# Two gate and up tiles move from the attention's filler to the seven-product phase, with a two-rate filler and later stores

## The chip, the cores and the metric

The kernel runs on one core of a Trainium2 chip. The core has a tensor engine (PE in the profile, with its weight loads as PEld), a vector engine (DVE), a scalar engine (ACT), GpSimd (POOL), and SyncE (SP), whose queue issues nearly all DMAs here. Each engine works through its own instructions in the order written and waits on semaphores for the others. The metric is device microseconds of one execution, the median of several runs; lower is better.

## The reference

One transformer block with a sequence of 2048 and a width of 640, in float32. Normalised tokens go through a causal attention with a window of 256 (32 heads of 20) and, in parallel, through a gated feed-forward part of width 1728; both are added to the input.

```python
xn = _layernorm(x, axis=-1)
return x + _A_ref(xn, A_wqkv, A_wo) + _B_ref(xn, B_w_gate, B_w_up, B_w_down)
...
scores = jnp.einsum("bhqd,bhkd->bhqk", q, k) * (Dh ** -0.5)
mask = (idx[:, None] - idx[None, :] >= 0) & (idx[:, None] - idx[None, :] < W)
p = _softmax(jnp.where(mask[None, None], scores, -1e9), axis=-1)
o = jnp.einsum("bhqk,bhkd->bhqd", p, v)
...
g = jnp.einsum("bsd,df->bsf", x, w_gate)
u = jnp.einsum("bsd,df->bsf", x, w_up)
return jnp.einsum("bsf,fd->bsd", _gelu(g) * u, w_down)
```

## The kernel before

Every large product is done with float32 operands split into a high and a low part, so that one product of depth 640 takes 3 x 5 = 15 matmuls of 128x128 weights against 512 tokens (`dense_steps`, L107; its matmuls are L111). The tokens stand in four chunks of 512 (`c` = 0 to 3). The work falls into four stretches.

First the normalisation and transposition, with the first query and key tiles and values. Then the attention, in 32 units: unit `u` is four heads (group `g = u // 4`) by one chunk (`c = u % 4`). Then the seven-product phase, which computes gate and up tiles. Last the output products.

The attention is written as a hand-made order (`attention`, L822). A unit has 14 slots. In each slot the program first does what was put off to that slot (`defer`), then what the tables say: pairs of row maxima at slots 0, 4 and 8 (`BURSTS`, `max_pair`, tile `ps_m`), score tiles and their exponentials at slots 2, 4, 6, 8 and 10 (`SCORES`, `exp_piece`, tiles `ps_e` and `P`), at slot 0 the product of the previous unit's probabilities with the values (`av_unit`, tile `ps_o`), and at slots 9 and 12 the loads of keys and queries for the unit three later (`load_stack`, tiles `ks` and `qs`). The queries of unit `u + 3` are first read by the maxima at slot 4 of the next unit, six slots after their load. The mask is cut into `P` by POOL (`clear`, L597 and L600) one slot after the last exponential of a group of four. A group of four score tiles is one of three pieces X, Z and Y in that order; the AV product uses X first, and in a first chunk (`c` = 0) Y directly after it.

At the end of each slot `pull_fill` takes from a queue of dense matmuls, the filler, until `RATE / NS` of them have been issued. The filler holds the remaining query and key tiles (`proj_qk`, 15 matmuls for a tile and chunk, tile `ps_d`), the values (`proj_v`, tile `ps_v`), and gate and up tiles (`gate_up_fill`, 2 x 15 matmuls for a tile and chunk). A list `sets` names their order, and `V1_AT` says behind which of them the 16 value projections of the second half of the heads stand. `NFA` is the number of gate and up tiles in the filler; the tiles `NFA` to 12 come in the seven-product phase. The half tile 13 is loaded by the filler and done at the phase's start.

A finished query or key tile goes ACT (`upper`), DVE (`middle`), ACT and POOL (`lower`) and then by `store` to DRAM (`qd`, `kd`), two slots after `lower`. An AV result goes ACT twice, POOL once (L630, tile `ob`, one slot later), and by its `store` to DRAM (`od`, `sd`) four slots after slot 0. These stores, the loads of `ks`, `qs` and weights (`wr`), and the stores of transposed-token sums (`td`) are all issued by SP, in the order written; a store that still waits for its data holds back all that stand behind it.

In the seven-product phase a tile and a pair of chunks take 54 matmuls in place of the 60 of `gate_up_fill`, since two chunks' gate and up share seven products of half depth (`gate_up_pair`, L952, matmuls at L970). DVE forms the sums of weights (`w_sums`), POOL the low parts of weights. Small jobs of DVE (`work`) hang between its parts.

Of the kernel before, what the change touches and what calls it, by code (L numbers as in the profile page):

```python
# [25 lines left out]
NF = 14  # L26
# [5 lines left out]
NS = 14  # L32
BURSTS = 0, 4, 8
SCORES = {2: range(0, 3), 4: range(3, 5), 6: range(5, 7), 8: range(7, 9), 10: range(9, 12)}
RATE = 34.05
V1_AT = "gu", 0, 3
VEARLY = 2
VLEAD = 40
POOL_SLOTS = 13, 0, 1, 2, 3, 4, 5, 6, 7
MXD = 6  # L40
KSLOT = 9
LAG = 3, 5, 4, 4, 4, 4, 3, 3, 4, 3, 2, 1, 1, 1
NFA = 4
HD = D // 2
HR = 5
NQD = 9
# [25 lines left out]
def block_kernel(ctx, tc, x, wqk, wv, wgu, wdo, wdl, out):  # L72
# [157 lines left out]
    def defer(n, fn, *a):  # L230
        if now[0] is None:
            fn(*a)
        else:
            at(now[0] + n, fn, *a)
# [17 lines left out]
    def save_qk(t, c, ps):  # L252
        pt = qkp.tile([128, 3, C], BF, name="pt", tag="pt")
        r = qkp.tile([128, C], F32, name="r", tag="r", bufs=1)
        dst = (qd if t < 5 else kd)[c]
        h, l = (2, 0) if t < 5 else (0, 2)

        def lower():
            nc.scalar.activation(pt[:, 1, :], r, AF.Copy)  # L259
            nc.gpsimd.tensor_tensor(out=pt[:, l, :], in0=r, in1=pt[:, 1, :], op=OP.subtract)  # L260
            defer(2, store)

        def store():
            a, end = t % 5 * 128, t % 5 * 128 + 128
            while a < end:
                g, b = divmod(a, 4 * DH)
                n = min(4 * DH - b, end - a)
                p = n - end + a + 128
                nc.sync.dma_start(dst[g, :, b:b + n, :].rearrange("p m t -> m p t"), pt[p - n:p])
                a += n  # L270
            done.add((t, c))

        def middle():
            nc.vector.tensor_tensor(out=r, in0=ps, in1=pt[:, h, :], op=OP.subtract)
            defer(lag(), lower)

        def upper():
            nc.scalar.activation(pt[:, h, :], ps, AF.Copy)
            late(middle)

        defer(1, upper)
# [333 lines left out]
    def av_unit(u):  # L615
        g, c = divmod(u, NC)
        halves, v = [bank("ps_o") for _ in range(2)], vtiles[g]
        todo = windows(c)
        for i, pair in enumerate(todo):
            for j in range(4):  # L620
                for h, bi, kb, col, q0, n in pair:
                    assert (id(v), kb) in done, (u, kb)
                    rows, w0_ = slice(64 * h, 64 * h + 64), kb * 84 + 21 * j
                    nc.tensor.matmul(halves[h][32 * j:32 * j + 32, q0:q0 + n], v[rows, w0_:w0_ + 32],  # L624
                                     pts[u, bi][rows, j, col:col + n], start=i == 0, stop=i == len(todo) - 1,
                                     skip_group_check=True, tile_position=(64 * h, 32 * j))
        ob, other = ap.tile([128, C], F32, name="ob", tag="ob", bufs=1), pts[u, 2][:, 0, :]
        nc.scalar.activation(ob, halves[0], AF.Copy)
        nc.scalar.activation(other, halves[1], AF.Copy)
        defer(1, lambda: nc.gpsimd.tensor_tensor(out=ob, in0=ob, in1=other, op=OP.add))  # L630

        def store():
            for j in range(4):
                nc.sync.dma_start(od[c].rearrange("(d h) t -> h d t", h=H)[4 * g + j], ob[32 * j:32 * j + DH, :])
            nc.sync.dma_start(sd[c][4 * g:4 * g + 4, :], ob[DH::32, :])

        defer(4, store)

    def load_gu(f):
        raws = []  # L640
# [60 lines left out]
                                   lambda k: xh[:, k, cs], lambda k: xl[:, k, cs], KT)  # L701
            defer(1, *((late, c4) if i else (c1,)))

    sets = [("qk", 1), ("qk", 2), ("qk", 3), ("gu", 0), ("qk", 4)]
    sets += [("gu", f) for f in range(1, NFA)] + [("gu", NF - 1)]
    pools = (wp, None), (hp, 2)
    rest = []

    def filler():
# [6 lines left out]
        for s, (kind, i) in enumerate(sets[:-1]):  # L716
            nxt = []
            after = sets[s + 1]
            for c in range(NC):
# [14 lines left out]
                if c in (1, 2) and c <= len(raws):  # L734
                    nxt.append(split_later(*pools[(s + 1) % 2], raws[c - 1]))
                if pending and (kind, i, c) == V1_AT:
                    pending = False
# [79 lines left out]
    def pull_fill(n):  # L817
        debt[0] += n
        while debt[0] > 0:
            debt[0] -= next(fill, 1.0)  # L820

    def attention():  # L822
# [18 lines left out]
        for u in range(NU + 1):  # L841
            for i in range(NS):
                T = now[0] = NS * u + i
                for fn, a in tick():
                    fn(*a)
                if i in BURSTS:
                    pull_max(2, T)
                if i == 0 and u:
                    av_unit(u - 1)
                    flush()  # L850
                    pull_max(2, T)
                for s in SCORES.get(i, ()) if u < NU else ():
                    exp_piece(u, s)
                flush()
                if i in POOL_SLOTS or T < NS:
                    release(2)
                if u + 3 < NU and i in (KSLOT, 12):
                    load_stack(u + 3, (int(i == KSLOT),))
                pull_fill(RATE / NS)
        while acts or idle:  # L860
            now[0] += 1
            for fn, a in tick():
# [491 lines left out]

    raws_next = {NFA + 1: load_gu(NFA + 1)}
    for j, f in enumerate(range(NFA, NF - 1)):
        end = f + 1 == NF - 1
# [92 lines left out]
    for n, (p, k) in enumerate(steps):  # L1450
        i = n % (NQD + 1)
# [74 lines left out]
```

## Time and profile before

| What | us |
|---|---|
| median of 3 runs | 1032.83 |
| the profiled execution | 1033.91 |
| its span, first to last instruction | 1032.2 |
| first AV product of the attention starts | 103.71 |
| last AV product starts | 552.09 |
| half tile 13 of gate and up starts | 555.12 |
| seven-product phase, first to last matmul | 568.76 to 789.26 |

A time is counted from the start of the span. The AV products mark the units: from one to the next is one turn of the 14 slots. In the profile's groups a name such as `ps_d<-xh,wqh` means that an instruction wrote `ps_d` and read the other two; a DMA `qs<-qd` moves from DRAM to `qs`, a DMA `qd<-pt` the other way. In the timeline the first column is the start and the second the length, "x5" counts merged instructions, and square brackets hold the idle time just before and what ended it. In the list of waits the columns are the total, the number of times and the longest.

### The profile page before, as it was taken

Reading aid. Unit: us, or ns where it says so; the run is one execution under the profiler, and the core shown is the slowest. Engines: PE = TensorE matmul, PEld = TensorE weight load, DVE = VectorE, ACT = ScalarE, POOL = GpSimd, SP = SyncE. Lnnn points to the kernel's source line nnn. Section 1 sums busy time; section 2 is a strip of 40 time slices with the busy share of each in tenths; the row PEclk is TensorE's granted clock in tenths of the full one; section 3 lists DMA queues with packets and bytes.
Section 4 is the critical chain, followed back from the end, with each engine's and each line's share of the span. In section 5 each row is a group of like instructions: output and inputs, shape, how many; then the busy total and the mean of one; then the engine's idle time right before and its main releaser. Section 6 shows DMA issues by size and latency. Waiting matters only on the chain.

```text
span 1032.2 us, 28689 instructions
## 1 busy us (share of the span) xinstructions
PE 1020.8 (99%) x10941; PEld 853.4 (83%) x10941; DVE 710.5 (69%) x2007; ACT 528.3 (51%) x1120; POOL 380.0 (37%) x543
## 2 busy tenths in 40 slices
PE   8999999999999999999999999999999999999998
PEld 8987676777788877777777888888888999999998
DVE  8844655666665566676644778776556879888887
ACT  4444667766676666766666423222224544333332
POOL 5232777877665578667664111110110000000000
PEclk9999999999999999999999999999999999999999
DMA  5642464655432364534324557767127864434342
GB/s 203 191 143 70 136 198 138 179 160 178 123 106 86 96 177 135 158 121 133 121 67 134 178 200 244 249 230 245 67 79 259 263 215 146 138 124 131 111 133 93
DMA packets 105203, 158.95 MB, mean 154 GB/s; under 512 B 15420, under 2 KB 60092, under 8 KB 105064
## 3 DMA queue, kind: packets, MB, share of 16 engines
q1 hardware_dynamic: 102680, 150.95, 46.0%
q10 hardware_dynamic: 2384, 6.16, 1.9%
q8 instruction: 86, 1.41, 0.6%
q14 instruction: 53, 0.43, 0.1%
HBM read 101.78 MB, written 54.92 MB: 152 GB/s over the span
## 4 chain that ended last, share of the span: by engine, by line
PE 85%; DMA 4%; DVE 4%; POOL 2%; ACT 1%; issue 1%; SPq 1%; DVEq 0%; ACTq 0%; POOLq 0%
PE ps_g L970 20%; PE ps_d L111 20%; PE ps L1237 18%; PE ps_e L584 7%; PE ps_v L111 7%; PE ps_o L624 6%; PE ps_m L525 4%; PE ps_g L111 1%; DMA qs<-qd 1%; PE ps_t L182 1%; POOL pt L260 1%; DVE at L1075 1%; DMA kd<-pt 1%; DVE wb L1075 1%; DMA hd<-hr 1%
## 5 line engine op out<-in xcount | busy, mean ns | idle before, releaser
L529 DVE CUSTOM_DVE_ANT_0 junk<-ps_m,mask 128x288 bf16<-128x288 f32 (+2 forms) x512 | 197.6, 441 | 127.0 <-PE ps_m L525 126.1
L586 ACT ACTIVATE P<-ps_e 128x512 f32<-128x512 f32 (+2 forms) x384 | 195.4, 574 | 54.8 <-PE ps_e L584 53.6
L1237 PE MATMUL ps<-wb,at 128*128 128x320 f32 x999 | 156.4, 309 | 0.8 <-DVE xr L1263 0.8
L1237 PEld LDWEIGHTS ps<-wb,at 128*128 128x128 f32 x999 | 148.9, 188 | 1.6 <-issue 1.0
L597 POOL TENSOR_SCALAR_AFFINE_SELECT P<-P 128x512 f32<-128x512 f32 x128 | 84.5, 661 | 86.2 <-ACT P L586 80.6
L584 PE MATMUL ps_e<-qs,ks 124*128 124x128 bf16 (+2 forms) x704 | 107.2, 277 | 1.6 <-DVE mx L529 1.3
L111 PE MATMUL ps_d<-xh,wqh 128*128 128x512 f32 x350 | 105.2, 410 | 0.0
L111 PE MATMUL ps_d<-xh,wql 128*128 128x512 f32 x350 | 105.1, 410 | 0.0
L111 PE MATMUL ps_d<-xl,wqh 128*128 128x512 f32 x350 | 105.1, 409 | 0.0
L1237 PE MATMUL ps<-wt,at 128*128 128x320 f32 x552 | 89.3, 309 | 0.4 <-DVE u L1075 0.4
L584 PEld LDWEIGHTS <-ks 124*128 124x128 bf16 x704 | 51.6, 98 | 40.7 <-issue 24.2
L1237 PEld LDWEIGHTS ps<-wt,at 128*128 128x128 f32 x552 | 82.9, 188 | 0.9 <-DVE u L1075 0.9
L1191 ACT ACTIVATE at<-ss 128x512 fp32r<-128x512 f32 x59 | 37.3, 632 | 89.9 <-DVE ss L1075 89.9
L104 POOL TENSOR_TENSOR wql<-wr,wqh 128x640 fp32r<-128x640 f32 x11 | 17.7, 1609 | 173.1 <-PE ps_g L970 129.3
L600 POOL TENSOR_SCALAR_AFFINE_SELECT P<-P 128x512 f32<-128x512 f32 x112 | 72.0, 653 | 16.5 <-ACT P L586 16.4
L624 PE MATMUL ps_o<-P,v 64*32 64x320 f32 (+5 forms) x2816 | 77.1, 347 | 0.2 <-POOL P L600 0.2
L111 PEld LDWEIGHTS ps_d<-xh,wql 128*128 128x128 f32 x350 | 63.9, 189 | 13.0 <-issue 2.1
L111 PEld LDWEIGHTS ps_d<-xh,wqh 128*128 128x128 f32 x350 | 63.2, 189 | 13.2 <-issue 2.6
L111 PEld LDWEIGHTS ps_d<-xl,wqh 128*128 128x128 f32 x350 | 63.6, 189 | 12.5 <-issue 2.3
L624 PEld LDWEIGHTS ps_o<-P,v 64*32 64x32 f32 x2816 | 66.9, 106 | 4.8 <-POOL P L600 1.4
L260 POOL TENSOR_TENSOR pt<-r,pt 128x512 bf16<-128x512 f32 x40 | 46.9, 1173 | 56.6 <-ACT pt L259 56.3
L525 PE MATMUL ps_m<-ks,qs 60*32 60x96 bf16 (+4 forms) x3008 | 61.0, 244 | 1.8 <-DMA qs<-qd 1.4
(196 smaller groups left out, 1906.9 us busy)
## 6 DMA issues: line engine op xcount, KB each, us to landing
hr<-hd SPq DMA_DIRECT2D x104, 128.0 KB
hd<-he SPq DMA_DIRECT2D x50, 256.0 KB
wr<-wgu SPq DMA_DIRECT2D x27, 320.0 KB
qs<-qd SPq DMA_DIRECT2D x64, 120.0 KB
ks<-kd SPq DMA_DIRECT2D x64, 120.0 KB
xi<-x SPq DMA_DIRECT2D x16, 320.0 KB
qs<-qd SPq DMA_DIRECT2D x64, 80.0 KB
ks<-kd SPq DMA_DIRECT2D x64, 80.0 KB
```

Source lines behind the costliest of these rows:

```text
L111: nc.tensor.matmul(ps, a(k), b(k), start=n == 0, stop=n == 3 * nk - 1)
L260: nc.gpsimd.tensor_tensor(out=pt[:, l, :], in0=r, in1=pt[:, 1, :], op=OP.subtract)
L525: nc.tensor.matmul(ps[32 * h:32 * h + 32, lo:hi], q[rows, j, q0:q0 + 32], keys, start=True, stop=True, tile_position=(64 * r, 32 * h))
L529: nc.vector.tensor_tensor_reduce(out=junk[:, 0:n], in0=ps[:, 0:n], in1=mask[:, 288 - n:288], scale=1.0, scalar=NEG, op0=OP.add, op1=OP.max ...
L584: nc.tensor.matmul(ps[:, col:col + n], k[0:QROWS, j, kc:kc + 128], q[0:QROWS, j, q0:q0 + n], start=True, stop=True)
L586: nc.scalar.activation(pt[:, j, lo:hi], ps[:, lo:hi], AF.Exp, scale=SCALE)
L597: nc.gpsimd.affine_select(out=a, in_=a, pattern=[[0, 4], [1, 128]], compare_op=OP.is_ge, fill=0.0, base=0, channel_multiplier=-1)
L600: nc.gpsimd.affine_select(out=a, in_=a, pattern=[[0, 4], [-1, 128]], compare_op=OP.is_ge, fill=0.0, base=-1, channel_multiplier=1)
L624: nc.tensor.matmul(halves[h][32 * j:32 * j + 32, q0:q0 + n], v[rows, w0_:w0_ + 32], pts[u, bi][rows, j, col:col + n], start=i == 0, stop=i ...
L970: nc.tensor.matmul(ps, i, j, start=first and n == 0, stop=n == len(work) - 1, skip_group_check=True)
L1191: nc.scalar.activation(hi[:, 3:7], s, AF.Copy)
L1237: nc.tensor.matmul(ps[bank][:, 0:HD], *work[bank][j], start=bank not in begun, stop=final[p, bank] == n and j == len(work[bank]) - 1, skip ...
```

## The change

`NFA` goes from 4 to 2, so gate and up tiles 2 and 3 leave the filler and join the seven-product phase, which has then eleven tiles. The one rate of 34.05 matmuls per unit becomes two, 32.0 in the first eight units and 24.6 behind them. The four query and key tiles now come one after the other, then gate and up tiles 0 and 1; the value projections of the second half stand in the first chunk of the fourth query and key tile. The stores of queries and keys come three slots after `lower` in place of two, those of AV results seven slots after slot 0 in place of four.

```diff
-RATE = 34.05
-V1_AT = "gu", 0, 3
+RATE = 32.0, 24.6
+V1_AT = "qk", 4, 0
...
-NFA = 4
+NFA = 2
...
-            defer(2, store)
+            defer(3, store)
...
-        defer(4, store)
+        defer(7, store)
...
-    sets = [("qk", 1), ("qk", 2), ("qk", 3), ("gu", 0), ("qk", 4)]
-    sets += [("gu", f) for f in range(1, NFA)] + [("gu", NF - 1)]
+    sets = [("qk", i) for i in range(1, 5)] + [("gu", f) for f in range(NFA)] + [("gu", NF - 1)]
...
-                pull_fill(RATE / NS)
+                pull_fill(RATE[u >= 8] / NS)
```

The order on SP, at the load of queries for unit 6 (in the profile at 145 to 150 us), before; the numbers in the names tell chunks and buffers apart:

```order
L269 DMA qd_84<-pt 64x3x512 x2
L238 DMA wr<-wqk 128x640 x2
L496 DMA qs_166<-qd_86 40x1024
L496 DMA qs_166<-qd_86 20x1024
L496 DMA qs_166<-qd_86 60x1024
L496 DMA qs_166<-qd_86 40x1024
L496 DMA qs_166<-qd_86 20x1024
L496 DMA qs_166<-qd_86 60x1024
L269 DMA kd_88<-pt 64x3x512 x2
```

The same place on SP now:

```order
L496 DMA qs_166<-qd_86 40x1024
L496 DMA qs_166<-qd_86 20x1024
L496 DMA qs_166<-qd_86 60x1024
L496 DMA qs_166<-qd_86 40x1024
L496 DMA qs_166<-qd_86 20x1024
L496 DMA qs_166<-qd_86 60x1024
L269 DMA qd_84<-pt 64x3x512 x2
L238 DMA wr<-wqk 128x640 x2
L760 DMA td_103<-tx 128x256
L269 DMA kd_88<-pt 64x3x512 x2
```

The six parts of the query load have moved ahead of the query store and of the pair of weight loads. At the next pair of query and key weights, the last, SP now has this between the key load (its last part first) and the query load of unit 10:

```order
L496 DMA ks_171<-kd_90 60x1024
L238 DMA wr<-wqk 128x640 x2
L760 DMA td_103<-tx 128x256
L269 DMA qd_84<-pt 16x3x512
L269 DMA qd_84<-pt 80x3x512
L269 DMA qd_84<-pt 32x3x512
L496 DMA qs_167<-qd_86 40x1024
```

Here the weights, a store of sums and a store of queries in three parts come first. On PE, between the last score matmul of unit 20 and the maxima that stand ahead of its AV product, before:

```order
L584 LDWEIGHTS ks_169
L584 MATMUL ps_e<-qs_168,ks_169 128x384
L111 MATMUL ps_d<-xh_79,wqh 128x512 x2
L111 MATMUL ps_d<-xh_79,wql 128x512 x5
L111 MATMUL ps_d<-xl_83,wqh 128x512 x3
L525 LDWEIGHTS qs_167
```

And now:

```order
L584 LDWEIGHTS ks_169
L584 MATMUL ps_e<-qs_168,ks_169 128x384
L111 MATMUL ps_d<-xh_78,wqh 128x512 x3
L111 MATMUL ps_d<-xh_78,wql 128x512 x4
L525 LDWEIGHTS qs_167
```

Seven filler matmuls stand in this gap in place of ten. Counted over whole units, PE has 32 filler matmuls of 512 columns in place of 34 between two AV products early, and 24 or 25 in place of 34 later; 6 in place of 2 stand behind the last AV product.

## The prediction

> **What bounds the kernel now.** First the top of the profile's page: how busy each engine is, and the clock that TensorE (PE) was granted.
>
> ```profile
> PE 1020.8 (99%) x10941; PEld 853.4 (83%) x10941; DVE 710.5 (69%) x2007; ACT 528.3 (51%) x1120; POOL 380.0 (37%) x543
> PEclk9999999999999999999999999999999999999999
> ```
>
> PE is busy nearly throughout at full clock, so the time is a count of PE work plus its few holes. Next, the view by windows, cut at three places: the first seven full units of the attention, the 24 units after them, and the seven-product phase with its nine tiles. Columns are the length, then busy time and instructions of PE, of its weight loads, of DVE, ACT and POOL, then clock, DMA share and GB/s.
>
> ```profile
> 103.71:208.86 105.15, 102.16 (x1693) 73.26 (x1672) 63.21 (x254) 73.12 (x146) 83.63 (x120) 1.00 0.56 164
> 208.86:552.09 343.23, 342.71 (x5677) 258.95 (x5653) 209.36 (x825) 229.01 (x509) 231.59 (x344) 1.00 0.42 127
> 568.76:789.26 220.50, 220.50 (x975) 182.58 (x974) 155.23 (x259) 70.29 (x131) 23.90 (x16) 1.00 0.55 189
> ```
>
> PE holes are 105.15 - 102.16 = 2.99 us in the first stretch, 343.23 - 342.71 = 0.52 in the second, none in the third. A unit takes 343.23 / 24 = 14.30 us late and 15.02 early. The chain of work that ended last gives the price of one 512-column matmul.
>
> ```profile
> 555.28 13.64 PE ps_g L111 x60
> 568.92 208.09 PE ps_g L970 x918
> ```
>
> 208.09 / 918 = 0.2267 us (13.64 / 60 = 0.2273 in the other loop). One tile of the seven-product phase is 108 such matmuls, 24.48 us; nine give 220.3 of the window's 220.50, so PE alone sets that phase.
>
> **The change, part by part.**
>
> Matmuls. Tiles 2 and 3 leave the filler: 2 tiles x 4 chunks x 30 = 240 matmuls less, at 0.2267 us -54.41 us. They come back as 2 x 108 = 216 in the seven-product phase, +48.97 us. Net -5.44 us, if PE remains the bound in both places. In the thin units the filler falls from 34 to 24 or 25 matmuls (the order shows it), so these should take about 14.30 - 9.5 x 0.2267 = 12.15 us.
>
> What those tiles do off PE. In the seven-product phase DVE is busy 155.23 / 9 = 17.2 us and ACT 7.8 us of a tile's 24.5, so two more tiles are covered by PE; their stores and loads go out at a DMA share of 0.55. If that cover went, DVE would have to lose over 7 us a tile. In the attention their conversions, activations and stores simply go. Cost nothing.
>
> The value projections of the second half start earlier in the filler, the first eight units get 32 instead of 34.05: the same matmuls at other places, priced in the sum above.
>
> The stores. Moving them issues nothing new, it moves queue positions on SP, where loads of queries stand behind them. What PE waits for in the attention:
>
> ```profile
> PE ps_m L525 <- DMA qs<-qd: 1.4, 3, 0.7
> PE ps_e L584 <- DVE mx L529: 1.3, 1, 1.3
> PE ps_m L525 <- DVE nm L539: 0.3, 1, 0.3
> PE ps_o L624 <- POOL P L600: 0.2, 1, 0.2
> ```
>
> Most of the first row is one place, shown by SP's and PE's timeline:
>
> ```profile
> 145.04 1.33 SPq L269 DMA_DIRECT2D qd<-pt  x2
> 146.41 1.12 SPq L238 DMA_DIRECT2D wr<-wqk  x2
> 147.63 2.28 SPq L496 DMA_DIRECT2D qs<-qd  x6
> ...
> 153.90 0.19 PE L525 MATMUL ps_m<-ks,qs 60*32 60x32 bf16 x1 [0.49 <-DMA qs<-qd]
> 154.74 0.52 PE L525 MATMUL ps_m<-ks,qs 60*32 60x32 bf16 x31 [0.65 <-DMA qs<-qd]
> ```
>
> The query load was issued by 149.91 and PE got it at 154.74, 4.83 us later, with two 320 KB weight loads just ahead of it. The new order puts the query load ahead of the store and of those weight loads. I take -1.14 us (0.49 + 0.65; between -1.14 and 0, if its landing was slow for another cause). But the order also puts the next pair of weight loads between the key and the query load of unit 10, where before the pair stood here:
>
> ```profile
> 250.39 0.86 SPq L238 DMA_DIRECT2D wr<-wqk  x2
> 251.35 2.18 SPq L496 DMA_DIRECT2D qs<-qd  x6
> ...
> 258.51 0.45 PE L525 MATMUL ps_m<-ks,qs 60*32 60x32 bf16 x32
> ```
>
> There 258.51 - 253.53 = 4.98 us were left and PE did not wait. At the new place a transposed-sum store and a three-part query store also stand ahead and the next unit is thin, so less is left. I take +1.1 us, the earlier place's wait, between 0 (this one's) and 2.5 (that wait and one more store of 1.33). The Trainium skill, "DMA: Bandwidth & Descriptors", section "Queues, rings and completion order", says that each DMA engine takes a ring's descriptors in order; by that rule the wait travels with the weight loads, -1.14 and +1.1, and without it both terms would be 0: the sum is the same within 0.1 us, but the places are not. The 4.83 us with the loads ahead agrees with the rule.
>
> The shorter way from the last exponentials to the AV product. Unit 20 (first chunk of a head group), from PE, ACT and POOL timelines:
>
> ```profile
> 392.78 0.83 PE L584 MATMUL ps_e<-qs,ks 124*128 124x128 bf16 x6
> 393.47 1.58 ACT L586 ACTIVATE P<-ps_e 128x512 f32<-128x512 f32 x3
> 395.17 0.64 POOL L597 TENSOR_SCALAR_AFFINE_SELECT P<-P 128x512 f32<-128x512 f32 x1 [1.89 <-ACT P L586]
> 395.76 0.64 POOL L600 TENSOR_SCALAR_AFFINE_SELECT P<-P 128x512 f32<-128x512 f32 x1
> 396.35 0.64 POOL L597 TENSOR_SCALAR_AFFINE_SELECT P<-P 128x512 f32<-128x512 f32 x1
> 396.09 1.95 PE L624 MATMUL ps_o<-P,v 64*32 64x320 f32 x62
> ```
>
> The last score tile is exponentiated and masked while PE works off filler and starts AV. In a first chunk the second group of 16 of the 64 AV matmuls needs the first two selects; it comes about 0.5 us after 396.09, at 396.6, and they end at 396.40. That leaves 0.2 us. The filler in this gap falls from 10 matmuls to 7, 0.68 us, so PE would wait some 0.45 us. Where it falls from 9 to 7 the loss is 0.23 less. Over the six thin first-chunk units I take 0.25 each, +1.5 us, between 0 and 6 x 0.45 = 2.7. In the other chunks the last tile is needed only after 64 of 96 matmuls, a microsecond later: 0.
>
> The remaining holes stay. The 1.3 us row is this:
>
> ```profile
> DVE r L274 <- POOL pt L260: 4.1, 1, 4.1
> 175.69 1.13 PE L584 MATMUL ps_e<-qs,ks 124*128 124x128 bf16 x6 [1.34 <-DVE mx L529]
> ```
>
> DVE stood 4.1 us behind a late POOL there, in a unit that keeps a dense filler: 0, between -2.37 (all other holes, 3.51 - 1.14) and the rival C below.
>
> Sum: -54.41 + 48.97 - 1.14 + 1.1 + 1.5 = -3.98 us. The profiled execution has 1033.91 us around its span of 1032.2; it becomes 1029.9. The median shown is 1032.83, 1.08 less, so the forecast is 1028.9 us.
>
> **Rivals.**
>
> A is the forecast, 1025 to 1031.5 us.
>
> B: the moved stores free SP, and the holes vanish without new ones: 1032.83 - 5.44 - 3.51 = 1023.9, up to 1025. For it: a query load now follows its key load directly in most early units. Against it: the 1.34 us hole came from POOL, and the thin gap above is new.
>
> C, on the other side: query loads land too late in thin units that still convert queries and keys. The chance comes from these rows:
>
> ```profile
> 409.95 3.60 SPq L496 DMA_DIRECT2D qs<-qd  x6
> 416.11 0.38 PE L525 MATMUL ps_m<-ks,qs 60*32 60x32 bf16 x28
> ```
>
> Issued by 413.55, first used at 416.11: 2.56 us were left, and enough. From the slot of that load to its use are six slots, and each loses 0.68 matmul: 6 x 0.68 x 0.2267 = 0.92 us. The AV store's later slot adds five issues just ahead of the key load, too. If ten such units lost 1 us each, the time is 1028.9 + 10 = 1038.9; from 0.4 us each on, the change is a loss. Against it: later query and key stores no longer stand ahead of the query load, which took 3.60 us instead of 2.2 here. 1031.5 to 1040.
>
> D: another engine holds the thin units at the old length. POOL was busy 231.59 of 343.23 us, 67%; in 343.23 - 24 x 2.15 = 291.6 us the same work is 79%, and it loses tile splits besides. DVE goes from 61% to 72%, but it is held at places where POOL works:
>
> ```profile
> 400.14 1.21 DVE L539 SCALAR_TENSOR_TENSOR nm<-mx,nm 128x16 bf16<-128x16 f32 x1
> 400.01 1.30 POOL L630 TENSOR_TENSOR ob<-ob,P 128x512 f32<-128x512 f32 x1
> ```
>
> A 16-element instruction took 1.21 us and ended as POOL's addition did. If each of 24 units held DVE by 1.21 us more, that is 29 us in 291.6 - 209.36 = 82 idle. So D needs far more than the trace shows. Its price, if the thin units kept 14.30 us: 1028.9 + 24 x 2.15 = 1080. It is a loss over 2% from 1 us per unit on. The Trainium skill, "SBUF — State Buffer", section "Who interferes with whom", says that a VectorE instruction with two SBUF inputs and a GpSimd one that reads SBUF shut each other out for a whole instruction; by that rule a denser attention meets such pairs more often, which is D's mechanism. The row above agrees.
>
> That the tiles save nothing (24 matmuls fewer, but slower ones) is excluded by 0.2267 against 0.2273.
>
> **How the numbers follow.** A 0.62, B 0.11, C 0.22, D 0.04, and 0.01 for a gain over 2% (20.7 us) by something unseen. The time is A's, 1028.9 us. The range 1024 to 1036 leaves out D, the unseen gain, B's lowest edge and C above 1036, some 0.15 together. A, B and C lie within 2% of 1032.83, about what a measurement of this kernel can tell from no change: faster 0.01, same 0.95, slower 0.04.
>
> **What would show it.** Right: late units of 12.1 to 12.4 us between AV products, eleven tiles of 24.5 us, no PE wait near the second pair of query and key weights, one there of about a microsecond at the pair after, and waits of PE on POOL's selects in first chunks of thin units. Wrong: PE holes of more than 8 us in the attention (C), units over 13 us with a full POOL or DVE (D), holes under 1 us (B), or a tile of the last kind that isn't 24.5 us.

## The result, and the profile after

| | before | after |
|---|---|---|
| median | 1032.82 us (6 runs) | 1041.48 us (6 runs, 1039.31 to 1044.86) |
| ratio after to before, 95% interval | | 1.0081 (1.0067 to 1.0096) |
| the profiled execution, its span | 1033.91, 1032.2 | 1039.58, 1037.8 |

The change makes the kernel 0.8% slower. That lies within the 2% band, but on the other side of the forecast and outside its range. The profiled execution is 5.67 us longer; the forecast for it was 4 us shorter, so 9.7 us have to be explained. Of the six runs of the kernel before, one took 1249.1 us and is not in the ratio.

First the engines on the page of the changed kernel, to be held against the row of before: busy time, share and instructions.

```profile
PE 1021.1 (98%) x10917; PEld 846.7 (82%) x10917; DVE 719.8 (69%) x2029; ACT 524.5 (51%) x1120; POOL 372.3 (36%) x527
```

PE has 24 matmuls fewer, as the change says, and no less busy time: a matmul that stands still inside PE is counted as busy in this row, so it can't tell where the time went. The view by windows can. It is cut at the same events as before: the first seven full units, the 24 thin units behind them, and the seven-product phase, now eleven tiles.

```profile
103.13:204.94 101.81, 99.01 (x1680) 70.83 (x1659) 60.50 (x253) 71.72 (x144) 82.94 (x120) 1.00 0.55 157
204.94:506.90 301.96, 296.83 (x5450) 214.62 (x5426) 194.11 (x802) 211.61 (x481) 218.94 (x324) 1.00 0.46 135
524.80:794.50 269.70, 269.70 (x1190) 223.02 (x1190) 182.29 (x304) 83.82 (x158) 29.86 (x20) 1.00 0.48 166
```

The third row answers to 220.50 us before: 49.2 us more, as predicted, with no hole. The first is 105.15 - 101.81 = 3.34 us shorter. The second is 343.23 - 301.96 = 41.27 us shorter, 12.58 us for a unit where 12.15 was forecast. It holds the miss. No engine is near its end there: POOL is busy 73%, ACT 70%, DVE 64%. The next two fences cut this stretch into units 7 to 11, 12 to 17 and 18 to 30, in the changed kernel and in the kernel before.

```profile
204.94:270.01 65.07, 63.02 (x1184) 44.41 (x1163) 42.36 (x178) 45.58 (x97) 52.85 (x83) 1.00 0.59 176
270.01:343.20 73.19, 73.16 (x1463) 60.10 (x1440) 44.67 (x204) 51.71 (x150) 47.09 (x69) 1.00 0.40 117
343.20:506.90 163.70, 160.64 (x2854) 110.11 (x2828) 107.08 (x420) 114.33 (x234) 119.00 (x174) 1.00 0.43 128
```

```profile
208.86:281.59 72.73, 72.31 (x1225) 52.62 (x1204) 46.45 (x184) 48.22 (x100) 52.50 (x78) 1.00 0.50 151
281.59:367.04 85.45, 85.45 (x1527) 71.18 (x1504) 48.21 (x209) 56.14 (x159) 51.71 (x84) 1.00 0.34 99
367.04:552.09 185.05, 184.94 (x2977) 135.15 (x2951) 114.70 (x433) 124.65 (x251) 127.38 (x185) 1.00 0.43 130
```

A unit saves (72.73 - 65.07) / 5 = 1.53 us in the first part, (85.45 - 73.19) / 6 = 2.04 in the second and (185.05 - 163.70) / 13 = 1.64 in the third; the forecast was 2.15 everywhere. The middle units have values as filler, and nothing of theirs goes through the conversions of query and key or gate and up tiles. They are nearly as thin as the others (5.40 us of filler in a unit against 4.97 in the third part, by the sum explained below), came out nearly as forecast, and have 0.03 us of holes. The others have 2.05 and 3.06 us.

What PE waits for in the attention, after:

```profile
PE ps_m L525 <- DMA qs<-qd: 4.2, 6, 0.9
PE ps_o L624 <- POOL P L600: 1.3, 2, 1.0
PE ps_m L525 <- DVE nm L539: 0.7, 2, 0.4
PE ps_e L584 <- DVE mx L529: 0.3, 1, 0.3
```

Idle time alone is short of the miss, so I summed something that needs no model of a matmul's end: the time from each matmul's start to the next one's, by what the two are: both filler; both AV products or maxima; anything and then a score matmul; all the rest. Over the 24 thin units the four sums make up the whole stretch (us, worked out from the traces; the kernels below the second are experiments).

```text
                                    stretch  filler  AV and maxima  scores  other
before                               343.23  173.13     70.13       65.98   33.99
after                                301.96  122.14     75.92       69.73   34.16
first-chunk order                    301.74  121.82     76.11       69.97   33.84
sums stored later                    301.71  121.82     75.37       69.96   34.57
maxima later                         302.34  121.83     76.92       69.39   34.19
maxima later, order                  302.36  121.89     75.31       69.70   35.46
before, with both                    345.76  172.93     72.46       65.99   34.38
addition on DVE                      303.40  122.30     74.89       70.58   35.63
middle later                         304.73  121.87     79.87       67.08   35.92
middle and maxima later, order       301.30  122.11     76.76       68.75   33.69
queries sooner                       303.75  121.87     76.48       70.55   34.85
queries sooner, order                302.29  121.92     76.03       69.99   34.34
before, addition on DVE, order       343.33  173.27     70.25       65.76   34.05
```

The filler saved 173.13 - 122.14 = 50.99 us for 228 matmuls, 0.2236 us each: the price was right. It was given back by the attention's own work: AV products and maxima 5.79 us, scores 3.75, other 0.17, in all 9.7 us where the prediction had allowed 2.6.

The chain of work that ended last says the same in another way. Between 360 and 400 us of the span before (units 17 to 20 there), PE's own pieces made up 37.8 + 13.7 + 10.2 + 6.9 = 68.6% of it (filler, scores, AV products, maxima). After, its three largest there are 5.8, 4.0 and 3.7%, and from 359.92 to 387.67 us, through units 19, 20 and 21, the chain has no piece of PE at all: it runs through POOL, SP, two query loads and a store of AV results. The end of this piece (start, length, engine, line; "issue" is time with no wait that the profile shows):

```profile
378.06 1.25 POOL wql L660 x3
379.32 1.13 POOL pt L260
380.45 0.02 issue
380.47 0.33 SPq L269
380.79 0.05 issue
380.84 1.41 SPq L269
...
383.85 3.69 DMA qs<-qd
387.54 0.14 issue
387.67 0.35 PE ps_m L525 x13
```

Three pieces of the loss can be read from single places. The first is a query load. In these rows it stands on SP behind a key store (L269) that waits for POOL, which splits weights (L660) first; PE waits 0.95 us for these queries. The place that the prediction named is of this kind. On PE and on SP, at unit 7:

```profile
202.89 1.74 SPq L238 DMA_DIRECT2D wr<-wqk  x2
204.73 0.36 SPq L760 DMA_DIRECT2D td<-tx  x1
205.19 1.44 SPq L269 DMA_DIRECT2D qd<-pt  x3
206.74 2.60 SPq L496 DMA_DIRECT2D qs<-qd  x6
...
210.53 0.17 PE L525 MATMUL ps_m<-ks,qs 60*32 60x32 bf16 x1 [0.49 <-DMA qs<-qd]
211.50 0.45 PE L525 MATMUL ps_m<-ks,qs 60*32 60x32 bf16 x31 [0.80 <-DMA qs<-qd]
```

The wait is 1.29 us; the old place, in unit 3, has none any more. The second piece is the score tiles. PE, then DVE, at unit 18:

```profile
351.48 0.44 PE L525 MATMUL ps_m<-ks,qs 60*32 60x288 bf16 x16
353.23 1.13 PE L584 MATMUL ps_e<-qs,ks 124*128 124x128 bf16 x6
...
352.11 0.69 DVE L274 TENSOR_TENSOR r<-ps_d,pt 128x512 f32<-128x512 f32 x1 [1.66 <-ACT pt L278]
352.72 0.45 DVE L529 CUSTOM_DVE_ANT_0 junk<-ps_m,mask 128x288 bf16<-128x288 f32 x1
```

The same DVE instructions at unit 18 before:

```profile
375.40 0.69 DVE L274 TENSOR_TENSOR r<-ps_d,pt 128x512 f32<-128x512 f32 x1 [0.50 <-ACT pt L278]
376.79 0.46 DVE L529 CUSTOM_DVE_ANT_0 junk<-ps_m,mask 128x288 bf16<-128x288 f32 x1 [0.70 <-PE ps_m L525]
```

There the subtraction (L274) was over 0.7 us before DVE got its maxima. After the change, the maxima were ready for DVE by about 351.9. DVE stood idle at the head of its queue for ACT's copy of a finished tile, and read them from 352.72 on. Maxima and score tiles share a ring of six banks (`bank`), so the six score matmuls took 1.13 us in place of 0.83 (unit 20 before, in the prediction), with nothing marked as idle: a score matmul can start only when DVE has read the maxima in its bank. Over the stretch DVE's waits of L274 for ACT's copies grew from 7.9 to 12.3 us. The third piece is the first-chunk AV product. POOL's selects and PE, unit 24:

```profile
420.59 0.64 POOL L597 TENSOR_SCALAR_AFFINE_SELECT P<-P 128x512 f32<-128x512 f32 x1 [1.90 <-ACT P L586]
421.18 0.64 POOL L600 TENSOR_SCALAR_AFFINE_SELECT P<-P 128x512 f32<-128x512 f32 x1
421.76 0.64 POOL L597 TENSOR_SCALAR_AFFINE_SELECT P<-P 128x512 f32<-128x512 f32 x1
...
420.94 2.34 PE L624 MATMUL ps_o<-P,v 64*32 64x320 f32 x64
```

The selects came during the product instead of ahead of it. From its first start to its last end it took 2.01 us in each first chunk before, and 2.04, 2.01, 2.19, 2.20, 2.34 and 2.14 after: 0.86 us in all six.

### The profile page after: what moved, and what is told of

Read it like the earlier page. It is cut to its first block, busy times and chain, and to the rows that moved or that the text cites. A ratio compares the mean times of both kernels' runs of the same rounds, so it can differ in the third digit from the quotient of the medians.

```text
span 1037.8 us, 28688 instructions
## 1 busy us (share of the span) xinstructions
PE 1021.1 (98%) x10917; PEld 846.7 (82%) x10917; DVE 719.8 (69%) x2029; ACT 524.5 (51%) x1120; POOL 372.3 (36%) x527
## 3 DMA queue, kind: packets, MB, share of 16 engines
q8 instruction: 86, 1.41, 0.6%
## 4 chain that ended last, share of the span: by engine, by line
PE 81%; DMA 4%; DVE 4%; ACT 4%; POOL 3%; issue 2%; SPq 1%; ACTq 0%; POOLq 0%; DVEq 0%
PE ps_g L969 25%; PE ps L1236 18%; PE ps_d L111 13%; PE ps_v L111 7%; PE ps_e L584 6%; PE ps_o L624 5%; PE ps_m L525 3%; ACT P L586 2%; DMA qs<-qd 2%; PE ps_g L111 1%; POOL P L600 1%; PE ps_t L182 1%; SPq L496 1%; DVE at L1074 1%; POOL pt L260 1%
## 5 line engine op out<-in xcount | busy, mean ns | idle before, releaser
L586 ACT ACTIVATE P<-ps_e 128x512 f32<-128x512 f32 (+2 forms) x384 | 195.1, 576 | 37.8 <-PE ps_e L584 35.6
L597 POOL TENSOR_SCALAR_AFFINE_SELECT P<-P 128x512 f32<-128x512 f32 x128 | 82.5, 646 | 64.9 <-ACT P L586 64.5
L104 POOL TENSOR_TENSOR wql<-wr,wqh 128x640 fp32r<-128x640 f32 x13 | 20.8, 1601 | 217.3 <-PE ps_g L969 192.8
L111 PE MATMUL ps_d<-xh,wqh 128*128 128x512 f32 x270 | 83.7, 414 | 0.0
L111 PE MATMUL ps_d<-xl,wqh 128*128 128x512 f32 x270 | 83.6, 415 | 0.0
L111 PE MATMUL ps_d<-xh,wql 128*128 128x512 f32 x270 | 83.5, 414 | 0.0
L600 POOL TENSOR_SCALAR_AFFINE_SELECT P<-P 128x512 f32<-128x512 f32 x112 | 71.8, 651 | 8.7 <-ACT P L586 7.8
L624 PEld LDWEIGHTS ps_o<-P,v 64*32 64x32 f32 x2816 | 62.8, 106 | 11.7 <-POOL P L600 5.6
L998 ACT ACTIVATE hr<-hr 128x512 f32<-128x512 f32 x22 | 13.9, 632 | 111.2 <-DVE hr L972 111.2
L525 PE MATMUL ps_m<-ks,qs 60*32 60x96 bf16 (+5 forms) x3008 | 62.0, 244 | 5.0 <-DMA qs<-qd 4.2
L969 PE MATMUL ps_g<-xh,wql 128*128 128x512 f32 x198 | 66.3, 389 | 0.0
L969 PE MATMUL ps_g<-xl,wqh 128*128 128x512 f32 x198 | 66.3, 389 | 0.0
```

The costliest lines, as they stand in the source:

```text
L111: nc.tensor.matmul(ps, a(k), b(k), start=n == 0, stop=n == 3 * nk - 1)
L525: nc.tensor.matmul(ps[32 * h:32 * h + 32, lo:hi], q[rows, j, q0:q0 + 32], keys, start=True, stop=True, tile_position=(64 * r, 32 * h))
L586: nc.scalar.activation(pt[:, j, lo:hi], ps[:, lo:hi], AF.Exp, scale=SCALE)
L597: nc.gpsimd.affine_select(out=a, in_=a, pattern=[[0, 4], [1, 128]], compare_op=OP.is_ge, fill=0.0, base=0, channel_multiplier=-1)
L600: nc.gpsimd.affine_select(out=a, in_=a, pattern=[[0, 4], [-1, 128]], compare_op=OP.is_ge, fill=0.0, base=-1, channel_multiplier=1)
L969: nc.tensor.matmul(ps, i, j, start=first and n == 0, stop=n == len(work) - 1, skip_group_check=True)
```

## The experiments

Times are medians, and a ratio is to runs of the kernel before on the same chip. The changed kernel stands at 1.0081. What each theory says is told with its experiment. One execution of each kernel was profiled; the last phase of the program, behind the seven-product phase, varied by itself between 241.7 and 245.9 us where nothing there had been edited (counted from the last matmul's start of that phase), so the thin stretch says more on a theory than the total. One thing more lengthens a profile. In seven of the twenty profiles the granted clock fell to half for 3.41 us, once or twice, which costs about 1.7 us each time (an estimate: half of 3.41; the row is in the last section) and makes 0.998 of the mean clock of a whole execution. In three of them this lies in the thin stretch: stores back, addition on VectorE alone, and middle later with the order.

**Stores back to their old slots.** Are the later stores the cause?

```diff
-            defer(3, store)
+            defer(2, store)
...
-        defer(7, store)
+        defer(4, store)
```

> The changed kernel with the stores of queries and keys again two slots, and those of AV results again four slots, behind. Theory T1 (the thin filler itself uncovers latencies: selects of first chunks, query loads, scores behind maxima; the stores matter little): 1038 to 1046 us, thin units 12.4 to 12.8 us as in the changed kernel. Rival T2 (the moved stores are what costs, by SP's order): 1028 to 1034 us, thin units near 12.2.

1039.99 us (1035.36 to 1041.75), ratio 1.0056 (1.0033 to 1.0079). Still slower than before, and the thin stretch took 305.72 us, some 304.0 without its half-clock time, no less than with late stores. The stores don't make the loss.

**Late stores in the kernel before.** The same edit the other way round, in the kernel with the dense filler.

> The kernel before with only the stores moved (three and seven slots). T1: 1029.5 to 1034 us, since ten matmuls per unit more cover them. T2: 1037 us or more.

1032.74 us, ratio 1.0002 (0.9987 to 1.0017). By themselves they do nothing: the thin stretch's counterpart took 342.98 us.

**First-chunk order.** The AV product of a first chunk uses X, Z, Y, so that the piece that is masked last is read last.

```diff
-        pairs = [(0, 0), (-2, -2), (2, -1), (-1, 2), (1, 1), (3, 3)] if c else [(d, d) for d in range(4)]
+        pairs = [(0, 0), (-2, -2), (2, -1), (-1, 2), (1, 1), (3, 3)] if c else [(d, d) for d in (0, 2, 1, 3)]
```

> The changed kernel; in first chunks the AV product takes its key blocks in the order 0, 2, 1, 3 in place of 0, 1, 2, 3, so that piece Y, masked last, is used last. T1: the wait of about 0.8 us in each of the six thin first-chunk units goes, and some of the one in unit 0: 5 to 6 us less, 1035.5 to 1037 us. If the wait only moves to the next one: 1040 to 1042.

1038.57 us, ratio 1.0046 (1.0028 to 1.0064). Its edit works: all first-chunk AV products of the thin stretch are at 2.01 us but unit 8's 1.96. The stretch is 301.74, no shorter. PE in unit 20 shows why:

```profile
368.50 1.95 PE L624 MATMUL ps_o<-P,v 64*32 64x320 f32 x62
...
371.48 0.83 PE L584 MATMUL ps_e<-qs,ks 124*128 124x128 bf16 x6
...
374.77 0.45 PE L525 MATMUL ps_m<-ks,qs 60*32 60x32 bf16 x31 [1.41 <-DMA qs<-qd]
```

AV product and scores run at the old lengths, PE comes to the maxima sooner, and waits 1.41 us there for queries. The selects are a real loss, of 0.86 us in all six first chunks where the expectation had 0.8 us in each, and taking it away hands the time to the next chain.

**Sums stored later.** The stores of token sums (L760) stand on SP ahead of query loads and wait for POOL; four slots later they should find their data ready.

```diff
-            defer(4, lambda: nc.sync.dma_start(td[p][i][:, k, half * w:half * w + w], t))
+            defer(8, lambda: nc.sync.dma_start(td[p][i][:, k, half * w:half * w + w], t))
```

> The changed kernel with the stores of transposed-token sums put off by eight slots in place of four, so that SP doesn't stand at them in front of key and query loads (SP waited 29.9 us there for POOL). If the late query loads come from SP's queue: PE's waits for queries (4.2 us) fall by half or more, 1037 to 1039.5 us. If they come from the landing time of the transfers: no change, 1040 to 1043.

1044.06 us, ratio 1.0103 (1.0081 to 1.0124); stretch 301.71. No gain. The total is no loss of the edit either, as far as is known: all four executions were granted a mean clock of 0.998 or less.

**Maxima later.** Without the extra burst ahead of the first unit, every query is first read ten slots after its load in place of six.

```diff
-        pull_fill(GAP / 2)
-        pull_max(2, now[0])
-        pull_fill(GAP / 2)
+        pull_fill(GAP)
```

> The changed kernel with the stream of row maxima started one burst of two pairs later, so that a unit's queries are first read ten slots after the slot of their load in place of six; nothing else moves. Theory T1b (of the 10 us that the 24 thin units take too long, query loads that land after their first use are about half, and hold back the rest): PE's waits for queries, 4.2 us, go to under 0.5, the 24 thin units take 295 to 299 us in place of 302, the time is 1035 to 1039. Rival T3 (the waits for queries only stand in for SP or POOL being short of time, so that the wait turns up at the next use): the 24 units stay at 300 to 303 us and the time at 1039 to 1043.

1037.79 us, ratio 1.0036 (1.0023 to 1.0048). PE's waits for queries in the attention fell from 4.2 to 1.5 us, but the stretch is 302.34: the edit has a price of its own, as the second run of the next group shows.

**Maxima later and first-chunk order,** in the changed kernel, and the same two in the kernel before.

> The changed kernel with the later maxima and with the AV product's order 0, 2, 1, 3 in first chunks. T1: both waits gone, 3 to 5 us more than the later maxima alone: the 24 thin units at 291 to 296 us, 1030 to 1035. T3: 300 us or more, 1037 or more.

> The kernel before with the same two edits. T1: only its holes of 3.5 us can go, 1029.5 to 1032.5. T3: the same as before, 1032 to 1034. It shows whether the tiles' move pays once the waits are gone: by the matmul count the changed kernel with both edits should then be 5.4 us below this one.

The changed kernel: 1036.91 us, ratio 1.003 (1.0015 to 1.0045). The kernel before: 1038.52 us, ratio 1.0039 (1.0021 to 1.0058), with a stretch of 345.76 in place of 343.23, so the edits cost 2.5 us there. PE's query waits in the stretch, with both edits in the changed kernel:

```profile
PE ps_m L525 <- DMA qs<-qd: 0.3, 1, 0.3
```

The 291 to 296 us of T1 are missed by far: with the select and query waits nearly gone from the stretch, the profile has 1.1 us of waits of filler and 0.7 of maxima there for which it names no cause. With the same edits on both sides the thin filler saves 345.76 - 302.36 = 43.40 us of 51.04 in the filler: the loss is 7.6 us, 2 less than the 9.7 without them. The medians, 1036.91 against 1038.52, don't show that the change has stopped being a loss: nine of the ten executions of the edited kernel before were granted 0.998 or less, none of the changed kernel's was, and with 1.7 us taken off for its half-clock time the profiled execution before (1038.3) is level with the one after (1036.75). Queries and selects are a part of the loss; the scores, 65.99 against 69.70, stand as high as ever.

**Rates.** Denser filler in units 8 to 11 and from 20 on, thinner in the value units between.

```diff
-RATE = 32.0, 24.6
+RATE = 32.0, 28.6, 20.0, 26.8
...
-                pull_fill(RATE[u >= 8] / NS)
+                pull_fill(RATE[(u >= 8) + (u >= 12) + (u >= 20)] / NS)
```

> The changed kernel with its filler spread otherwise over the thin units: 28.6 per unit in units 8 to 11, 20.0 in units 12 to 19 (values, where POOL and SP have little to do), 26.8 behind them; the sum is the same. If the loss belongs to units whose filler itself needs POOL, DVE and SP: it falls by a third or more, the 24 units take 296 to 300 us, 1035 to 1039. If it only depends on how much filler a unit has on the average: 301 to 304 us, 1040 to 1043.

1039.63 us, ratio 1.0035 (1.0015 to 1.0056); stretch 303.70 with six filler matmuls (1.4 us) more in it. The total loss stays, as the second theory said, but it moves. A unit's filler and all the rest of it, in us, from the same sums as above (units 11, 17 and 18 change their kind of filler):

```text
                         before          changed        rates
                      filler  rest    filler  rest   filler  rest
units 7 to 10          7.18   7.49     4.96   8.09    5.89   7.41
units 12 to 16         7.43   6.75     5.40   6.76    4.32   7.53
units 19 to 30         7.15   7.05     4.98   7.58    5.50   7.43
```

With 28 to 30 filler matmuls, units 7 to 10 lose nothing any more, though their filler is the same kind of work (all but 6 matmuls). The value units, which lost nothing, lose 0.8 us each at 30 or 31 value matmuls in place of 37 or 38. Units 19 to 30, with 26 or 27 in place of 24 or 25, got back 0.15 of 0.53 us each. So the loss follows the thickness of the filler, and how much a unit needs depends on what its filler does: 5.40 us are enough for a value unit, 5.50 are not for one with conversions.

**The addition of AV results on VectorE.** If a late POOL were behind everything, 1.3 us less of it in each unit should shorten the stretch.

```diff
-        defer(1, lambda: nc.gpsimd.tensor_tensor(out=ob, in0=ob, in1=other, op=OP.add))
+        defer(1, lambda: nc.vector.tensor_tensor(out=ob, in0=ob, in1=other, op=OP.add))
```

> The changed kernel with the addition of the two AV halves (1.28 us a unit on POOL) done by DVE (some 0.7 us). Theory T4: in thin units POOL's lateness is the common root of the waits (selects of first chunks, stores that SP stands at with query loads behind them, two-input instructions of DVE that POOL holds up), which is why removing one wait only let the next show: the 24 thin units fall from 302 to 293 to 298 us, 1033 to 1038. Rival T5: DVE is as short as POOL, so the work only changes place: 301 us or more, 1040 or more.

1039.31 us, ratio 1.0059 (1.0036 to 1.0082); stretch 303.40, some 301.7 without its half-clock time, where theory T4 wanted 293 to 298. POOL's load is not the common root.

**The same with the first-chunk order,** in the changed kernel and in the kernel before.

> The changed kernel with that addition on DVE and with the AV product's order 0, 2, 1, 3 in first chunks. T4: the select waits that are left go too, 291 to 296 us for the 24 units, 1029 to 1035. T5: 300 us or more, 1037 or more.

> The kernel before with the same two edits: there POOL has the time, so 1029.5 to 1034 by either theory. Under T4 the changed kernel with the two edits ends 2 to 5 us below this one (the matmul count says 5.4); under T5 it stays above.

Changed kernel: 1039.59 us, ratio 1.0069 (1.0048 to 1.0091), with a stretch of 302.73: T4's 291 to 296 is missed. Kernel before: 1031.23 us, ratio 0.998 (0.9971 to 0.999), faster than both kernels of this study. Its windows, the first seven units and the 24 behind them:

```profile
103.81:206.51 102.70, 102.19 (x1693) 73.48 (x1672) 63.61 (x261) 72.85 (x146) 75.59 (x113) 1.00 0.58 167
206.51:549.84 343.33, 342.74 (x5678) 258.85 (x5654) 207.58 (x849) 228.84 (x509) 200.01 (x321) 1.00 0.42 127
```

All of its gain lies in the first row: 105.15 fell to 102.70, holes from 2.99 to 0.51 us. In the dense filler a hole that is closed stays closed.

**Middle later.** DVE's subtraction (L274) one slot later, so that it doesn't stand behind ACT's copy of the same slot; alone, with the order, and with order and later maxima.

```diff
-            late(middle)
+            defer(1, late, middle)
```

> The changed kernel, with DVE's subtraction of a finished query, key or gate/up tile (r, L274) put off by one slot, so that it no longer stands in DVE's queue directly behind ACT's copy of the same slot. Theory T6 (in thin units DVE's in-order queue stands behind ACT's results, so row maxima and scores come late): PE's waits at the scores (excess over the usual spacing 4.5 us) fall to about 1.5, the 24 thin units from 301.96 to 297 to 300 us, the time to 1035 to 1039 us. Rival T7 (the slots are just shorter than every chain's latency, whichever engine holds it): the thin units stay at 301.5 us or more, and the stores and query loads, one slot later, lose elsewhere.

> The same, and in a first chunk the pieces in the order X, Z, Y for the AV product as well, so that Y, masked last, is read last. T6: the gain of the two edits adds up, thin units 294 to 298 us, time 1033 to 1036 us. T7: thin units at 301.5 us or more as with the order alone (301.74), time 1037 to 1040 us.

> The same two edits, and the maxima without their early burst, so that queries are first read ten slots after their load. With all three covers in place T6 expects 297 to 300 us for the thin units (the late maxima alone cost 2.5 us over 24 units in the kernel before) and 1032 to 1035 us; T7 expects 302 us as with the late maxima and the order alone, and 1035 to 1038 us.

1048.32, 1046.71 and 1042.72 us; ratios 1.015 (1.0119 to 1.0181), 1.0139 (1.0119 to 1.016) and 1.0094 (1.0072 to 1.0116). The edit also makes the work ahead of the first AV product 4.2 us longer (it starts at 107.33 in place of 103.13), so the totals aren't fair to it; the stretch is: 304.73, 306.63 (some 304.9 without its half-clock time) and 301.30. T6 said two things. The scores do come sooner: their sum fell from 69.73 to 67.08. DVE, then PE, at the place shown above, with the edit alone:

```profile
358.34 0.46 DVE L529 CUSTOM_DVE_ANT_0 junk<-ps_m,mask 128x288 bf16<-128x288 f32 x1 [1.40 <-PE ps_m L525]
...
359.48 0.83 PE L584 MATMUL ps_e<-qs,ks 124*128 124x128 bf16 x6
```

DVE now waits for PE, and the six score matmuls take 0.83 us. But the stretch got longer, since queries and keys are stored a slot later:

```profile
PE ps_m L525 <- DMA qs<-qd: 6.5, 6, 1.7
```

That row stood at 2.6 us in the same stretch of the changed kernel. So the mechanism is shown, and that it holds the others is not.

**All three in the kernel before.**

> The kernel before with three edits: the subtraction one slot later, the addition of AV results on VectorE in place of GpSimd, and the order X, Z, Y in first chunks. With the last two alone it took 1031.23 us. If DVE behind ACT cost anything in the dense filler too, 1029 to 1031 us; if the dense filler covered that already, 1031 to 1032 us.

1037.91 us, ratio 1.0048 (1.0031 to 1.0064): 4.1 us of the loss are the later start (107.95 in place of 103.81), and the dense stretch took 344.89. A miss.

**Queries sooner.** The load of queries at slot 11 in place of 12; alone, with the order, and in the best version.

```diff
-                if u + 3 < NU and i in (KSLOT, 12):
+                if u + 3 < NU and i in (KSLOT, 11):
```

> The changed kernel with the loads of queries at slot 11 in place of 12, one slot after the scores that free their buffer. In the changed kernel spacings above 0.12 us inside the maxima sum to 4.52 us over the 24 thin units, against 0.47 before, most of them behind such loads. Theory T8 (the late query loads are a loss of their own): these 4 us go, the thin units take 298 to 299.5 us, the time 1036 to 1038.5 us. Theory T7 (slots shorter than several latencies at once; a wait that is taken away shows up at the next chain): the spacings inside the maxima fall by 2 us or more, those at the scores or the AV products rise, and the thin units stay within 301 to 303 us.

> The same, and the pieces of a first chunk in the order X, Z, Y for the AV product, which by itself took the select waits away and lengthened the query waits. T8: both covers together give what the order alone could not, thin units 296.5 to 299 us, time 1034.5 to 1037 us. T7: thin units 300.5 us or more.

> The kernel before with the addition of AV results on VectorE, the order X, Z, Y in first chunks, and the loads of queries at slot 11. With the first two alone it took 1031.23 us, with hardly a wait left in the attention. T8 and T7 both expect no more than the rest of the query waits, 0.5 us: 1030 to 1032 us.

1038.0 us, ratio 1.0051 (1.0028 to 1.0074); 1037.17, 1.0043 (1.0028 to 1.0059); 1031.29, 0.9972 (0.9953 to 0.9991). T8 falls: the stretch is 303.75 and 302.29. T7 isn't met as it was put either: it wanted the spacings inside the maxima down by 2 us, and they stayed, 4.97 us after 4.52, and the 303.75 lie above its 303. In the loads behind the edit the slot isn't what counts. At unit 21 SP now had this:

```profile
382.36 1.47 SPq L269 DMA_DIRECT2D kd<-pt  x2
383.93 2.24 SPq L496 DMA_DIRECT2D qs<-qd  x6
```

The query load still went out behind a key store. In the best version the sooner loads made no difference that these runs can tell (0.9972 and 0.998, with intervals that overlap); its profiled stretch was 345.09 us, against 343.33 without them.

## Why the prediction was wrong

By its own steps:

- *Eleven tiles at 24.48 us, +48.97:* right. The phase is 49.2 us longer, without a hole, and its extra DVE, ACT and DMA work was covered.
- *Each filler matmul less is worth 0.2267 us:* right as a price (0.2236 measured over the thin stretch). Only the filler's own sum shows it.
- *The weights' wait, -1.14 and +1.1:* right at both places. Unit 3 has no wait, unit 7 has one of 0.49 + 0.80 = 1.29 us. But in the first seven units other waits took the place of the one removed: 0.69 + 0.94 us for queries in unit 4, and 1.0 us for a select in unit 0. They are 3.34 us shorter where 14 matmuls and the wait made 4.3.
- *The select waits, +1.5:* right in kind, 0.86 us in size (1.2 by the spacings in the table).
- *"The remaining holes stay": 0.* This is the step that failed. It looked at the one 1.34 us hole, found its unit still dense, and gave the thin units nothing. But with 24 or 25 filler matmuls in a unit, DVE's late reading of maxima holds score tiles in many units: scores cost 3.75 us more, and no term had them; the run with DVE's subtraction a slot later got 2.65 of these back. In the dense filler of before DVE stood for ACT's copies too, but at unit 18 it was done before the maxima came. And what the thin filler uncovers goes away where it is made thicker: at 28 to 30 matmuls units 7 to 10 have no loss left.
- *The query waits:* the term counted one place. The trace showed that others were near, 2.56 us of slack against 0.92 us that thinning takes away, and that stood in rival C with a chance of 0.22. In the stretch the list of waits names 2.6 us for queries, of which unit 7 has 1.29; ten units at 1 us were too many.
- *The median, 1.08 us below the profiled execution:* it lies 1.9 above, some 3 us of the 12.6 by which the forecast missed the median. Both executions with a mean granted clock of 1.0 took 1039.31 and 1039.58 us; the four at 0.998 took 1041.17 to 1044.86. A single half-clock time, at about 1.7 us (the estimate above), would make 0.998 and a part of this; these executions have no profile kept, and the rest stays open. Among the 81 runs of the kernel before that stand beside the experiments, 12 were at 0.998 or less.
- *The rest* of the 5.79 us of AV products and maxima: 0.64 us in the AV product of unit 30, no first chunk, where a select came late (2.54 us before, 3.18 after), about 0.1 in other units, 0.7 where the maxima wait for DVE, and some 1.2 us around the maxima that no row names.

Rival C had the sign and, by a different sum, about the time (1038.9), which is part luck; its range ended at 1040, below the median. Its own mechanism is a part; the scores and the selects, which it didn't have, cost more than its query waits. B fell: holes in the first 31 units went from 3.51 to 2.80 + 5.13 us. D fell: no engine holds the units, and with POOL relieved of 1.3 us a unit nothing was gained.

What is shown: the loss comes with the thin filler, and goes where the filler is made thicker; in the changed kernel it falls on units with conversions in their filler, and with other rates on value units as well; it lies in the attention's own matmuls, and three chains carry it, each of which an edit could shorten (queries to 0.3 us of waits, first-chunk AV products to 2.01, scores to 67.08). What is shown as well is that none of these edits shortens the stretch by more than 0.7 us, alone or in the combinations tried: 301.3 to 306.6 us in every variant, and at most some 304.9 without the half-clock times. What stays open is what sets that length. That several chains are too long for the slots at once fits every run, but no run had all of them short, and T7's own number for the maxima wasn't met. A likely next suspect, not tried: the way from POOL over SP to the queries, where a load stands behind a store that waits for POOL while POOL splits weights.

## What to carry to other kernels

In a schedule written by hand, filler is cover as well as work. Before thinning it, take every chain that ends at the busy engine (loads, row statistics, masks), set its smallest slack in the trace against what thinning takes from it, and put all that come out short into the sum together: here they were priced as one term and one rival, and they came all at once. The cover that a unit needs depends on what else its filler sets going, so a rate is best set part by part, each against its own chains. Work that moves to a phase where PE has no holes keeps its price (49.2 us against 48.97 here), so the question is always what the place that it left was covering; and a closed wait pays in full only where the next chain has slack, as in the best version here, which closed holes in the dense part.

## What the runs showed of the hardware

A tiny instruction on VectorE can be held for microseconds by GpSimd. The groups of DVE on 16 elements, first in the kernel before, then in the version of it whose additions are on VectorE (busy us, mean ns of one):

```profile
L538 DVE TENSOR_SCALAR nm<-mx 128x16 bf16<-128x16 f32 x32 | 21.7, 679 | 1.1
L539 DVE SCALAR_TENSOR_TENSOR nm<-mx,nm 128x16 bf16<-128x16 f32 x32 | 17.4, 544 | 1.1
```

```profile
L538 DVE TENSOR_SCALAR nm<-mx 128x16 bf16<-128x16 f32 x32 | 7.6, 239 | 1.1
L539 DVE SCALAR_TENSOR_TENSOR nm<-mx,nm 128x16 bf16<-128x16 f32 x32 | 6.8, 213 | 1.1
```

With 32 additions gone from GpSimd, the same instructions take 239 and 213 ns in place of 679 and 544, 24.7 us of DVE time in all, about what the additions themselves take on DVE (24.3 us). The longest, in the changed kernel at unit 21, spanned GpSimd's addition and ended with the instruction behind it:

```profile
385.73 2.24 DVE L538 TENSOR_SCALAR nm<-mx 128x16 bf16<-128x16 f32 x1
...
385.30 0.72 POOL L756 TENSOR_TENSOR tx<-tx,xl 128x256 f32<-128x256 f32 x1
385.99 1.27 POOL L630 TENSOR_TENSOR ob<-ob,P 128x512 f32<-128x512 f32 x1
387.22 0.72 POOL L756 TENSOR_TENSOR tx<-xh 128x256 f32<-128x256 f32 x1
```

It ran from 385.73 to 387.97, and the three GpSimd instructions together from 385.30 to 387.94. The instruction of L538 reads one tile only. The Trainium skill, "SBUF — State Buffer", section "Who interferes with whom", says that VectorE and GpSimd exclude each other for a whole instruction on the shared port pair, through a second SBUF input of VectorE or its two-port modes, which a `tensor_scalar` can enter when its operands meet the conditions. That agrees for L539, which has two inputs; for L538 the runs show the hold, three instructions long, and not by which of these ways.

A short hole on PE can be followed by a time at half clock. The window of it in the changed kernel with the addition on VectorE, whose last figures are granted clock, DMA share and GB/s:

```profile
376.90:380.31 3.41, 3.29 (x42) 2.13 (x43) 2.20 (x9) 1.28 (x3) 1.36 (x3) 0.50 0.44 146
```

In such a time the run with other rates started its filler matmuls 0.43 us apart, in place of 0.23. The seven profiles have ten of these times ahead of the program's last microseconds, each 3.41 us long, and each began 1.6 to 3.2 us after the start of a PE hole of 1.4 to 2.6 us. Not every such hole has one: behind the 1.59 us hole at 827.46 in the changed kernel the clock stayed at 1.0. So a hole that a thinner cover opens can cost more than its own length, in some executions and not in others.
